# Window attention and its gradients on one core: start-up loads, one weight product and the crossed copies are rearranged

## The chip, the cores and the metric

The kernel runs on one core of a Trainium2 chip. A core has a matrix engine (TensorE, PE in the profile), VectorE (DVE), ScalarE (ACT), GpSimd (POOL) and SyncE (SP), each with an instruction stream of its own. SP, ACT and POOL also issue DMA transfers; SPq, ACTq and POOLq are their issues in the profile. PEld is TensorE loading the stationary operand of its next products. The metric is the device time of one execution in microseconds; less is better.

## The reference

An image of 256 x 256 tokens with 384 channels is cut into windows of 8 x 8 tokens. Each window attends within itself, with one head; then the gradients of all three inputs are formed for a given gradient of the output. Everything is bf16 outside the sums.

```python
# per window (64 tokens), C = 384
qkv = xw @ wqkv                       # q, k, v
p = softmax(q @ k.T * C ** -0.5)
o = (p @ v) @ wo
# outputs: o, and d/dx, d/dwqkv, d/dwo for grad_out
```

## The kernel before, in words

The windows are taken eight at a time: a "quad" is four pairs of vertically adjacent windows (QUAD = 4, 128 tokens a pair), and there are 128 quads. The weights are multiplied out first: A = w_q w_k^T (scaled) and B = w_v w_o, with the transposes AT and BT, so that scores, values and gradients come from x and the output's gradient (dq in the code, with d for its columns) in one product each.

The order of the instructions is the order of the program on all five engines (a manual schedule): each engine takes its instructions as the code lists them and waits where operands or buffers are not ready. All PSUM tiles come from one ring of eight banks.

The main loop (line 490) has 129 iterations i. Each first issues on SP the transposing DMAs dT and xT of quad i+2 (`load_turn`, L151), then `to_tokens` of quad i (L188, tile tok from zy); then `step(c, b, a, ahead)` with c = quad i-1, b = quad i, a = quad i+1 and ahead = quad i+4 lays out one step:

- scores of b on PE (tile sd), then eight products u and v of b (`uv`), copied out of PSUM by ACT, with the softmax parts (`soft`, mostly DVE) in between;
- for the first four quads and the last ("crossed" quads) `stack` has ACT copy P into the tile cr (L246), `soft(…, 5)` has DVE write the gradient of the scores beside it (L239), and `turn` transposes cr by a DMA on SP into PS (L264). cr has one buffer. For the others DVE transposes (L267, L271);
- the projections of a (`project`, three z and three y, copied by ACT at L176 and L178), gathered by DVE into zy (L184);
- from i = 4 on, sums for the weight gradients (tiles pg and ph);
- the attention of c (`attend`, L296): four slots of products pw, pu, po and pd, which need tok and PS of quad c; their results are copied by ACT and DVE and stored by POOL.

`load` (L142 and L144) issues a quad's gradient on POOL and its x on SP, four transfers each.

Ahead of the loop: `fetch_weights` issues w_v and w_o on SP and ACT; seven warm-up products run on PE; POOL builds the identity and clears the accumulator GF_acc; `load_first` issues the gradient of quad 0 on SP and ACT in turn, then `fetch_rest` (w_q on SP, w_k on ACT), then x of quad 0 on SP, and has POOL copy one column of the gradient's last part to the tile spare (L136), so that POOL's loads of quads 1 and on wait until that part has landed. PE then turns w_v, forms BT (`weight_product`, L110), turns the gradient, w_q, projects, turns w_k and x, forms A, and so on. `weight_product` fills one bank after another. w_o is turned for the end of the kernel (`turn_blocks(woT_sb, wo_sb)`) after step 1.

Of the kernel before, what the change touches and what calls it, by code (L numbers as in the profile page):

```python
# [8 lines left out]
ACT = mybir.ActivationFunctionType  # L9
ALU = mybir.AluOpType  # L10
AX = mybir.AxisListType
BF16 = mybir.dt.bfloat16
F32 = mybir.dt.float32

P = 128
WIN = 8
WT = WIN * WIN
QUAD = 4
# [5 lines left out]
def kernel(  # L24
# [21 lines left out]
    nc = tc.nc  # L46
    _, H, W, C = x.shape
    CK = C // P
    J = 3 * C
    JK = J // P  # L50
    scale = float(C) ** -0.5
# [3 lines left out]
    qp = ctx.enter_context(tc.tile_pool(name="qp", bufs=2))  # L55
    sm = ctx.enter_context(tc.tile_pool(name="sm", bufs=2))
    ob = ctx.enter_context(tc.tile_pool(name="ob", bufs=8))
    ring = ctx.enter_context(tc.tile_pool(name="ring", bufs=8, space=bass.MemoryType.PSUM))
# [13 lines left out]
    def columns(k):  # L72
        return slice(k * C, (k + 1) * C)

    def fetch_weights():
        wo_in = wo.rearrange("(m p) n -> p m n", p=P)
        nc.sync.dma_start(out=w_sb[:, 0:2, columns(2)], in_=w_in[:, 0:2, columns(2)])
        nc.scalar.dma_start(out=w_sb[:, 2, columns(2)], in_=w_in[:, 2, columns(2)])
        nc.scalar.dma_start(out=wo_sb[:, 0:2, :], in_=wo_in[:, 0:2, :])
        nc.sync.dma_start(out=wo_sb[:, 2, :], in_=wo_in[:, 2, :])  # L80

    def fetch_rest():
        nc.sync.dma_start(out=w_sb[:, :, columns(0)], in_=w_in[:, :, columns(0)])
        nc.scalar.dma_start(out=w_sb[:, :, columns(1)], in_=w_in[:, :, columns(1)])

    def warm_up(n):
        zero = B_sb[:].rearrange("p m c -> p (m c)")[:, 0:4 * P]
        nc.vector.memset(zero, 0.0)
        for i in range(n):
            pt = ring.tile([P, 4 * P], F32, tag="r", name="warm")  # L90
            nc.tensor.matmul(pt[:], lhsT=zero[:, 0:P], rhs=zero, start=True, stop=True)

    def copy_out(i, out, in_):
        if i % 2:
            nc.scalar.copy(out=out, in_=in_)
        else:
            nc.vector.tensor_copy(out=out, in_=in_)
# [6 lines left out]
            copy_out(k, dst[:, k, :], pt[:])  # L104

    def weight_product(dst, left, right, sc):
        for mr in range(CK):
            pc = ring.tile([P, C], F32, tag="r", name="pc")
            for mc in range(CK):
                nc.tensor.matmul(pc[:], lhsT=left[:, mc, mr * P:(mr + 1) * P], rhs=right[:, mc, :],  # L110
                                 start=(mc == 0), stop=(mc == CK - 1))
            if sc is not None:
                nc.scalar.activation(out=dst[:, mr, :], in_=pc[:], func=ACT.Copy, scale=sc)
            else:
                copy_out(mr, dst[:, mr, :], pc[:])

    def weight_rest():
        turn_blocks(B_sb, BT_sb)
        turn_blocks(AT_sb, A_sb)

    def windows(ap, st, first, count=2):
        row, col = st["at"]
        return ap[0, row + WIN * first:row + WIN * (first + count), col:col + WIN, :]
# [4 lines left out]
    def load_first(st):  # L128
        st["xq"] = xq = grp.tile([P, QUAD, C], BF16, tag="xq", name="xq", bufs=2 * GQ + 5)
        st["dq"] = dq = qp.tile([P, QUAD, C], BF16, tag="dq", name="dq", bufs=6)  # L130
        for t in range(QUAD):
            (nc.sync, nc.scalar)[t % 2].dma_start(out=dq[:, t, :], in_=windows(grad_out, st, 2 * t))
        fetch_rest()
        for t in range(QUAD):
            nc.sync.dma_start(out=xq[:, t, :], in_=windows(x, st, 2 * t))
        nc.gpsimd.tensor_copy(out=spare[:, 0:1], in_=dq[:, QUAD - 1, 0:1])  # L136

    def load(st):
        st["xq"] = xq = grp.tile([P, QUAD, C], BF16, tag="xq", name="xq", bufs=2 * GQ + 5)
        st["dq"] = dq = qp.tile([P, QUAD, C], BF16, tag="dq", name="dq", bufs=6)  # L140
        for t in range(QUAD):
            nc.gpsimd.dma_start(out=dq[:, t, :], in_=windows(grad_out, st, 2 * t))  # L142
        for t in range(QUAD):
            nc.sync.dma_start(out=xq[:, t, :], in_=windows(x, st, 2 * t))  # L144
# [55 lines left out]
    def over_k(ap, n=P):  # L200
        return ap.unsqueeze(2).broadcast_to([n, QUAD, WT])

    def soft(st, step):
        sd = st["sd"]
        if step == 0:
# [35 lines left out]

    def stack(st):
        if st["crossed"]:
            st["cr"] = cr = qp.tile([P, QUAD, 2, WT], BF16, tag="cr", name="cr", bufs=1)
            for w, h in ((0, LO), (1, HI)):
                nc.scalar.copy(out=cr[h, :, w, :], in_=st["Pb"][h, :, :])  # L246

# [87 lines left out]
    def gf_rows(sts, f, ma):  # L335
        pw = ring.tile([P, C], F32, tag="r", name="pg")
        n = len(sts) * QUAD
        for i in range(n):
            st, t = sts[i // QUAD], i % QUAD
            product(pw[:], st["xq"][:, t, ma * P:(ma + 1) * P], st["UW"[f] + "q"][:, t, :], i == 0, i == n - 1)  # L340
        gf_add(f, ma, [pw])
# [23 lines left out]
    def attention(st):  # L365
        halves = gf_halves(*fill.pop(0)) if fill else iter(())
        for t in range(QUAD):
            attend(st, t)
            yield
            for k in range(QUAD):  # L370
                next(halves, None)

    def step(c, b, a, ahead):


        def on(st):
            return (lambda f, *r: f(st, *r)) if st is not None else (lambda f, *r: None)
        C_, B, A = on(c), on(b), on(a)
        if b is not None and c is None:
            weight_rest()  # L380
        B(scores)
        B(soft, 0)
        B(uv, 0, 0)
        B(uv, 0, 1)
        B(soft, 1)
        B(uv, 1, 0)
        B(uv, 1, 1)
        B(soft, 2)
        B(soft, 3)
        B(uv, 2, 0)  # L390
        B(uv, 2, 1)
        B(stack)
        B(uv, 3, 0)
        B(uv, 3, 1)
        B(soft, 4)
        for mo in range(CK):
            A(project, 0, mo)
        B(soft, 5)
        B(turn)
        if ahead is not None:  # L400
            load(ahead)
        A(gather, 0)
        for mo in range(CK):
            A(project, 1, mo)
        for rows in range(1 if a is not None else 2):
            if fill:
                gf_rows(*fill.pop(0))
        slots = attention(c) if c is not None else iter(())
        for t in range(QUAD):
            if t == 2:  # L410
                A(gather, 1)
            next(slots, None)
        for rest in slots:
            pass
# [5 lines left out]
    sts = [{"at": q, "i": i, "crossed": i <= GQ or i == n - 1} for i, q in enumerate(quads)]  # L420
# [41 lines left out]
    with tc.manual_schedule(engines=MANUAL):  # L462
        spare = sm.tile([P, 1], BF16, name="spare", bufs=1)
        fetch_weights()
        warm_up(7)
        make_identity(nc, ident[:])
        nc.gpsimd.memset(GF_acc[:], 0.0)
        load_first(sts[0])
        load(sts[1])
        load(sts[2])  # L470
        load_turn(sts[0])
        load_turn(sts[1])
        turn_blocks(wT[2], w_sb, 2 * CK)
        weight_product(BT_sb, wo_sb, wT[2], None)
        turn_on_pe(sts[0], "dq", "dT")
        turn_blocks(wT[0], w_sb, 0)
        for mo in range(CK):
            project(sts[0], 0, mo)
        turn_blocks(wT[1], w_sb, CK)
        turn_on_pe(sts[0], "xq", "xT")  # L480
        gather(sts[0], 0)
        weight_product(A_sb, wT[0], wT[1], scale)
        turn_on_pe(sts[1], "dq", "dT")
        for mo in range(CK):
            project(sts[0], 1, mo)
        gather(sts[0], 1)
        held = []
        last = None
        get = lambda i: sts[i] if 0 <= i < n else None
        for i in range(n + 1):  # L490
            if 0 <= i < n - 2:
                load_turn(sts[i + 2])
            if 0 <= i < n:
                to_tokens(sts[i])
            if i == 0:
                load(sts[AHEAD - 1])
            step(get(i - 1), get(i), get(i + 1), get(i + AHEAD))
            if i == 1:
                turn_blocks(woT_sb, wo_sb)
            if i > 0:  # L500
                held.append(sts[i - 1])
                sts[i - 1] = None
            if held and i == n:
                last = gf_final(held)
            elif len(held) == GQ:
                fill.extend((held, f, ma) for f in range(2) for ma in range(CK))
                held = []
        while fill:
            gf_rows(*fill.pop(0))
        weight_gradients(last)  # L510
# [30 lines left out]
```

## Time and profile before

| | us |
|---|---|
| median of three runs | 1905.82 |
| the three runs | 1900.98, 1905.82, 1908.59 |
| the profiled execution | 1906.89 |
| its span | 1905.1 |
| PE busy | 1892.1 |
| DVE, ACT, POOL busy | 1667.7, 1526.8, 861.8 |
| mean granted TensorE clock | 0.999 |

The span runs from the first to the last instruction that the profiler recorded; the device time holds 1.79 us more. Times of events are microseconds from the start of the span. A timeline row gives start, duration, engine, source line, operation, destination and source tile, count, and in brackets the idle time before it with what ended that. A row "PE 1892.1 (99%)" says how long an engine worked, as a share of the span; products on PE overlap, so a busy PE is not necessarily at its peak. By issue the DMA part lists, in the first 60 us, x loads of 96 KB landing 3.8 us after their issue in the median, POOL's gradient loads 4.2 us, the four gradient loads of quad 0 on SP and ACT 5.1 and 4.9 us, and the transposes of tok 6.8 us.

### The profile page before, as it was taken

The numbers are of one execution on the slowest core, as the hardware profiler recorded it, in microseconds if no ns is written. First come the engines' busy times: TensorE is split into PE (matmuls) and PEld (weight loads), VectorE is DVE, ScalarE is ACT, GpSimd is POOL, SyncE is SP. The second block draws the span as 40 slices with busy tenths as digits, with TensorE's granted clock in tenths as the row PEclk, the third lists the DMA queues.
The fourth block names the chain that finished last, engine by engine and source line by source line (L and its number), as shares of the span: only waits on it lengthen the run. The fifth ranks groups of instructions, "written<-read, shape, count | busy, mean of one in ns | idle before, by whom it ended". The sixth has DMA issues, their size and how long they took to land.

```text
span 1905.1 us, 57100 instructions
## 1 busy us (share of the span) xinstructions
PE 1892.1 (99%) x22333; PEld 1127.1 (59%) x22333; DVE 1667.7 (88%) x3613; ACT 1526.8 (80%) x3355; POOL 861.8 (45%) x1572
## 2 busy tenths in 40 slices
PE   9999999999999999999999999999999999999999
PEld 5565655655665566556555655665566556556655
DVE  5888888888888888888888888888888888888887
ACT  7877887888788888878887888788788878887884
POOL 4444444444454445444444544444445445444432
PEclk9999999999999999999999999999999999999999
DMA  9999999999999999999999999999999999999994
GB/s 208 218 226 204 219 222 230 217 217 216 223 220 214 222 216 219 218 210 228 216 217 206 228 217 223 217 219 214 220 221 219 217 212 222 223 216 221 195 202 104
DMA packets 949647, 408.34 MB, mean 214 GB/s; under 512 B 831232, under 2 KB 924864, under 8 KB 949376
## 3 DMA queue, kind: packets, MB, share of 16 engines
q1 hardware_dynamic: 873056, 253.08, 77.6%
q0 software_dynamic: 75072, 150.72, 31.4%
q8 instruction: 175, 2.87, 0.6%
q10 hardware_dynamic: 1248, 0.89, 0.2%
q14 instruction: 96, 0.79, 0.1%
HBM read 101.84 MB, written 101.84 MB: 107 GB/s over the span
## 4 chain that ended last, share of the span: by engine, by line
PE 96%; DMA 2%; ACT 1%; DVE 1%; issue 0%; DVEq 0%; ACTq 0%
PE pj L162 51%; PE pg L162 13%; PE ph L351 13%; PE sd L162 5%; PE pw L296 5%; PE pu L296 4%; PE po L296 4%; DMA tok<-zy 1%; PE pd L296 1%; DMA w_sb<-in_wqkv_dram 0%; DMA PS<-cr 0%; PE pe L429 0%; ACT yz L176 0%; ACT yz L178 0%; PE pt L103 0%
## 5 line engine op out<-in xcount | busy, mean ns | idle before, releaser
L316 POOL DMA_DIRECT2D out_dram<-o x512 | 274.5, 536 | 897.3 <-ACT o L300 885.3
L307 ACT CAST Wq<-pw 128x384 bf16<-128x384 f32 x506 | 244.0, 482 | 280.4 <-PE pw L296 280.3
L162 PEld LDWEIGHTS <-xT 128*128 128x128 bf16 x3072 | 291.7, 98 | 182.5 <-issue 0.5
L162 PE MATMUL pj<-B_sb,xT 128*128 128x384 bf16 x1536 | 333.4, 326 | 0.1
L162 PE MATMUL pj<-AT_sb,xT 128*128 128x384 bf16 x1536 | 333.3, 326 | 0.0
L142 POOL DMA_DIRECT2D dq<-in_grad_out_dram x508 | 268.8, 537 | 96.1 <-DMA out_dram<-d 38.3
L310 DVE CAST Uq<-pu 128x384 bf16<-128x384 f32 x512 | 283.1, 553 | 13.2 <-PE pu L296 1.1
L318 POOL DMA_DIRECT2D out_dram<-d x480 | 279.3, 582 | 15.4 <-ACT uq L256 6.8
L162 PE MATMUL pj<-dT,BT_sb 128*128 128x512 bf16 x1152 | 269.5, 379 | 0.0
L162 PE MATMUL pj<-xT,A_sb 128*128 128x512 bf16 x1152 | 269.5, 379 | 0.0
L296 PE MATMUL pd<-tok,ps 64*64 64x384 bf16 x2048 | 257.3, 327 | 1.9 <-DMA tok<-zy 1.5
L176 ACT CAST yz<-pj 128x512 bf16<-128x512 f32 x384 | 224.0, 587 | 36.7 <-PE pj L162 28.4
L300 ACT CAST o<-po 128x384 bf16<-128x384 f32 x512 | 249.8, 488 | 1.5 <-PE po L296 1.1
L256 ACT CAST vq<-pj 128x384 bf16<-128x384 f32 x512 | 247.0, 482 | 3.2
L256 ACT CAST uq<-pj 128x384 bf16<-128x384 f32 x512 | 244.3, 477 | 4.4 <-PE pj L162 2.5
L178 ACT CAST yz<-pj 128x512 bf16<-128x512 f32 x384 | 224.5, 588 | 22.8
L271 DVE STREAM_TRANSPOSE PS<-ps 32x256 bf16<-32x256 bf16 x492 | 214.5, 436 | 9.4
L162 PEld LDWEIGHTS <-xq 128*128 128x128 bf16 x1572 | 153.6, 98 | 115.3 <-issue 0.9
L351 PEld LDWEIGHTS <-xq 64*64 64x64 bf16 x6000 | 176.2, 107 | 67.7
L351 PE MATMUL ph<-Wq,xq 64*64 64x384 bf16 x3984 | 204.5, 322 | 0.0
L162 PEld LDWEIGHTS <-A_sb 128*128 128x128 bf16 x1152 | 112.7, 98 | 135.7
L162 PEld LDWEIGHTS <-BT_sb 128*128 128x128 bf16 x1152 | 112.7, 98 | 122.1
(93 smaller groups left out, 3060.0 us busy)
## 6 DMA issues: line engine op xcount, KB each, us to landing
xq<-in_x_dram SPq DMA_DIRECT2D x512, 96.0 KB, 4.0
out_dram<-o POOLq DMA_DIRECT2D x512, 96.0 KB, 4.0
dq<-in_grad_out_dram POOLq DMA_DIRECT2D x508, 96.0 KB, 5.9
out_dram<-d POOLq DMA_DIRECT2D x480, 96.0 KB, 4.6
out_dram<-d POOLq DMA_DIRECT2D x64, 48.0 KB, 5.1
tok<-zy SPq DMA_TRANSPOSE x128, 7.8
xT<-xq SPq DMA_TRANSPOSE x127, 7.2
dT<-dq SPq DMA_TRANSPOSE x126, 7.9
```

What stands on the lines that cost most here:

```text
L142: nc.gpsimd.dma_start(out=dq[:, t, :], in_=windows(grad_out, st, 2 * t))
L162: nc.tensor.matmul(out, lhsT=lhsT, rhs=rhs, start=start, stop=stop)
L176: ENG[EV["z"][mo]](out=yz[:, mo, :, 0:4:3, :], in_=pj[:])
L178: ENG[EV["y"][mo]](out=yz[:, mo, :, 1:3, :], in_=pj[:])
L256: cp(out=dst[:, t, :], in_=pj[:])
L296: nc.tensor.matmul(dst[o, :], lhsT=operand(st, lhs, t, h), rhs=operand(st, rhs, t, h), **flags)
L300: copies[EV[name][i]](out=sb[rows, :], in_=src[rows, :])
L307: copies[EV["W"][t] if st["i"] >= GQ else "DA"[t % 2]](out=st["Wq"][:, t, :], in_=pw[:])
L310: copies[EV["U"][t]](out=st["Uq"][:, t, :], in_=pu[:])
L316: nc.gpsimd.dma_start(out=windows(out_0, st, 2 * t), in_=o)
L318: nc.gpsimd.dma_start(out=windows(out_1, st, 2 * t - 1), in_=d if t else above[:])
L351: nc.tensor.matmul(dst[o, :], lhsT=st["xq"][h, t, ma * P + o.start:ma * P + o.stop], rhs=st["UW"[f] + "q"][h, t, :], start=(i == 0), stop= ...
```

## The change

There are five edits, all outside the steady part of the loop, save that the last quad is crossed too.

1. The remaining weights (w_q, w_k) are issued within `fetch_weights`, ahead of the gradient of quad 0.
2. The gradient of quad 0 is issued on POOL, four transfers, ahead of the clearing of GF_acc; the copy to spare follows the clearing.
3. `weight_product` takes three banks at once and runs the contraction in its outer loop, so the three banks are complete together; the copies follow.
4. `stack` comes after the last u and v products of its step, and cr has two buffers (the pool's default).
5. w_o is turned after step 0 instead of after step 1.

```diff
     def fetch_weights():
...
         nc.sync.dma_start(out=wo_sb[:, 2, :], in_=wo_in[:, 2, :])
-
-    def fetch_rest():
         nc.sync.dma_start(out=w_sb[:, :, columns(0)], in_=w_in[:, :, columns(0)])
         nc.scalar.dma_start(out=w_sb[:, :, columns(1)], in_=w_in[:, :, columns(1)])
...
     def weight_product(dst, left, right, sc):
+        pcs = [ring.tile([P, C], F32, tag="r", name="pc") for mr in range(CK)]
+        for mc in range(CK):
+            for mr in range(CK):
+                nc.tensor.matmul(pcs[mr][:], lhsT=left[:, mc, mr * P:(mr + 1) * P], rhs=right[:, mc, :],
+                                 start=(mc == 0), stop=(mc == CK - 1))
         for mr in range(CK):
-            pc = ring.tile([P, C], F32, tag="r", name="pc")
-            for mc in range(CK):
-                nc.tensor.matmul(pc[:], lhsT=left[:, mc, mr * P:(mr + 1) * P], rhs=right[:, mc, :],
-                                 start=(mc == 0), stop=(mc == CK - 1))
             if sc is not None:
-                nc.scalar.activation(out=dst[:, mr, :], in_=pc[:], func=ACT.Copy, scale=sc)
+                nc.scalar.activation(out=dst[:, mr, :], in_=pcs[mr][:], func=ACT.Copy, scale=sc)
             else:
-                copy_out(mr, dst[:, mr, :], pc[:])
+                copy_out(mr, dst[:, mr, :], pcs[mr][:])
...
         for t in range(QUAD):
-            (nc.sync, nc.scalar)[t % 2].dma_start(out=dq[:, t, :], in_=windows(grad_out, st, 2 * t))
-        fetch_rest()
+            nc.gpsimd.dma_start(out=dq[:, t, :], in_=windows(grad_out, st, 2 * t))
         for t in range(QUAD):
             nc.sync.dma_start(out=xq[:, t, :], in_=windows(x, st, 2 * t))
-        nc.gpsimd.tensor_copy(out=spare[:, 0:1], in_=dq[:, QUAD - 1, 0:1])
...
-            st["cr"] = cr = qp.tile([P, QUAD, 2, WT], BF16, tag="cr", name="cr", bufs=1)
+            st["cr"] = cr = qp.tile([P, QUAD, 2, WT], BF16, tag="cr", name="cr")
...
-        B(stack)
         B(uv, 3, 0)
         B(uv, 3, 1)
+        B(stack)
...
+        load_first(sts[0])
         nc.gpsimd.memset(GF_acc[:], 0.0)
-        load_first(sts[0])
+        nc.gpsimd.tensor_copy(out=spare[:, 0:1], in_=sts[0]["dq"][:, QUAD - 1, 0:1])
...
-            if i == 1:
+            if i == 0:
                 turn_blocks(woT_sb, wo_sb)
```

## The prediction

> **What bounds the kernel now.** I read the profile in this order: the page's first part, engine use by stage, the chain of work that ended last, then the timelines of ScalarE (ACT), the SP queue and TensorE over the first 100 us. First the page and five stages, cut where the behaviour changes (columns: stretch, length, busy time of PE, weight loads, DVE, ACT, POOL, then granted clock, DMA share, GB/s):
>
> ```profile
> span 1905.1 us, 57100 instructions
> ...
> PE 1892.1 (99%) x22333; PEld 1127.1 (59%) x22333; DVE 1667.7 (88%) x3613; ACT 1526.8 (80%) x3355; POOL 861.8 (45%) x1572
> ...
> 0.00:18.50 18.50, 15.96 (x125) 9.74 (x126) 5.90 (x17) 10.61 (x21) 12.94 (x27) 1.00 0.90 230
> 18.50:71.00 52.50, 47.65 (x420) 25.18 (x417) 39.76 (x93) 41.28 (x95) 16.17 (x30) 0.97 1.03 209
> 71.00:190.50 119.50, 117.76 (x1399) 70.40 (x1396) 103.52 (x225) 94.99 (x208) 54.72 (x100) 1.00 1.15 214
> 190.50:1821.00 1630.50, 1630.43 (x19468) 972.89 (x19471) 1450.48 (x3135) 1325.73 (x2911) 751.96 (x1371) 1.00 1.12 218
> ```
>
> From 190.5 to 1821 us PE is never idle, and its scores start every 14.56 us: 112 steps that no line of the change touches. All it can win is PE's idle time before 190.5 (2.54 + 4.85 + 1.74 = 9.1 us) and whatever the clock lost there. The stall the change aims at is step 2, on ACT and then PE:
>
> ```profile
> 46.40 0.48 ACT L256 CAST vq<-pj 128x384 bf16<-128x384 f32 x1
> 51.28 0.82 ACT L246 COPY cr<-ps 64x256 bf16<-64x256 bf16 x2 [4.40 <-DMA PS<-cr]
> ...
> 52.65 0.32 PE L296 MATMUL pw<-dq,ps 64*64 64x384 bf16 x1 [1.64 <-ACT uq L256]
> ...
> 54.00:56.00 2.00, 1.72 (x16) 0.51 (x16) 1.49 (x3) 2.00 (x5) 0.00 (x0) 0.73 1.18 235
> 56.00:58.00 2.00, 2.00 (x29) 1.62 (x28) 1.94 (x5) 1.69 (x5) 1.41 (x3) 0.50 1.16 218
> ```
>
> ACT stands 4.4 us before the crossed copy, because the one cr buffer is still being read by quad 1's transpose; the last uq and vq and all z and y copies queue behind it, PE idles 1.64 us, and then the clock falls to half. But the queue that feeds PE tells another story:
>
> ```profile
> 39.25 4.96 SPq L188 DMA_TRANSPOSE tok<-zy  x1
> 44.31 3.20 SPq L264 DMA_TRANSPOSE PS<-cr  x1
> 47.57 2.88 SPq L144 DMA_DIRECT2D xq<-in_x_dram  x4
> 50.68 1.45 SPq L151 DMA_TRANSPOSE dT<-dq  x1
> 52.17 1.86 SPq L151 DMA_TRANSPOSE xT<-xq  x1
> 54.14 3.98 SPq L188 DMA_TRANSPOSE tok<-zy  x1
> ...
> L188 SPq EVENT_SEMAPHORE  x4: 27/28/28, 54.1 to 98.9; - x4
> ...
> 84.65 11.45 DMA tok<-zy
> ...
> 172.31 13.57 DMA tok<-zy
> ```
>
> SP issues back to back from 14.53 us on, and its semaphore instructions ahead of a tok transpose last 28 ns: it waits for no engine. tok(1) leaves at 39.25, 12.1 us behind the start of its step (27.18); tok(4) at 84.65 is 13.6 and tok(10) at 172.31 is 13.4 behind (71.04 and 158.94). Those two, each needed by the attention of the step after, are the last two rows, from the chain that ended last: PE waited 1.52 us for tok(10) at 185.92. Only afterwards does SP catch up (12.4 us behind in step 12, 6.4 in step 22). So the start-up is bound by SP's transposes; a faster PE meets them sooner.
>
> **The change part by part.** The profiled execution took 1906.89 us, 1.79 more than its span and 1.07 above the median of 1905.82.
>
> *Loads.* w_q's block goes out on SP right after wo, at about 1.76 instead of 3.84 us, and w_k's on ACT at about 1.7 instead of 3.32: SP and ACT lose two gradient issues each (1.46 and 1.26 us). w_q took 5.9 us to land (9.74), and PE idled 1.34 us for it. It lands between 7.7 (same 5.9 us) and 9.7 (the same bytes share the same engines: 249 and 237 GB/s at 8 to 10 us); I take the middle, -0.7 us of PE idle, and keep 0 and -1.3. x of quad 0 starts on SP at about 2.2 instead of 4.75, but SP held back issues until older loads had landed (0.6, 0.5 and 0.3 us before the w_q block and x), so the third and fourth issue still wait for landings at 3.3 to 3.8, and the next quad's for w_q and w_k. I put x of quad 1 0.7 us earlier; this is the load for which SP's first transpose waited 1.5 us (12.9 to 14.4). That -0.7 shifts the whole SP chain; the bounds are -2.5 (all of x's advance) and 0 from this edit.
>
> *The gradient on POOL.* Four issues at 0.58 us (POOL's median there) from 1.31 to 3.6, then the 2.01 us clearing to 5.6, hidden: POOL stood until 7.61 for the gradient anyway. Gradient loads issued before 14 us took 3.3 to 5.3 us to land, so the last (issued near 3.0) lands at 6.3 to 8.3; before, POOL's copy to spare saw it at 7.61. Everything POOL issues next (20 gradient loads from 7.73) stands behind that copy and moves by -1.3 to +0.7; I take 0. By the Trainium skill (DMA: Bandwidth & Descriptors, Specifications) a load issued by GpSimd has its first byte after about 1 us against 0.6 from SP or ACT; by it the gradient would be 0.4 us later and the sum below 1905.5. No run here shows that figure: the rows have POOL's loads landing no later than SP's (4.2 in the median over 60 us against 5.1), under other traffic.
>
> *w_o w_v in three banks.* The same nine matmuls. For BT_sb the first bank is now complete after seven of them instead of three, but the last copy (7.81 to 8.37) stays: nothing. For A_sb, all three copies are ACT's: they began 0.2 us after the first bank (14.11; matmuls 0.163 apart from 13.42) and now begin at about 14.75, ending near 16.2 instead of 15.58. ACT's dT copies and the three y copies (16.40 to 18.28) queue behind and end up to 0.7 later; quad 0's scores wait for them. Between 0 (PE's B and AT turns stand until 18.66) and +0.7; I take +0.5, being nearer to ACT's queue.
>
> *Crossed copies last, two buffers.* In step 0 ACT waited 0.41 us for ps ahead of cr, with uq and vq behind it: -0.4. In step 1 it stood 1.82 us; the attention stage then took 5.04 us (36.68 to 41.72) against 3.89 in step 3 (67.15 to 71.04): -1.2. In step 2 the 4.4 us stand goes: 16.2 us become step 3's 12.5, -3.7, of which about 1.9 is the halved clock (54.5 to 58.3). Step 3 waited 0.45 with no PE idle: 0. In the last quad the copies end about 0.5 us later on ACT, at 1871.8, but DVE's half of cr is written until 1873.1 and is what the transpose waits for: 0; without that cover it would be +0.5.
>
> *w_o's turn a step earlier.* Nine transposes, 0.64 us of PE between steps 1 and 2 (41.72 to 42.36), move to the end of step 0, where PE waited 0.29 + 0.29 us and more for y copies (27.18 to 28.16). DVE's two turn copies (0.61) then stand before quad 1's row maximum, which had 0.32 us of slack: -0.4 net, bounds -0.64 and 0.
>
> PE alone: -0.7 + 0.5 - 0.4 - 1.2 - 0.4 - 3.7 = **-5.9 us**.
>
> **What is late next.** Step 2 would start at 40.2 (2.2 earlier) and its attention be due 8.6 later, at 48.8. It needs quad 1's turned P and S, issued at 44.31 behind tok(1) and landing 6.9 later, at 51.2: PE idles about 2.4 us there instead. Step 3 starts at 55.1 (57.0 if the clock halves again) instead of 58.56, so step 4 at 67.6 to 69.5, and its attention is due at 78.2 to 80.1; quad 3's transpose lands at 73.28 + 7.1 = 80.4. Step 5's attention began at 96.14 the moment tok(4) landed (84.65 + 11.45 = 96.10). From there PE stands where SP puts it: every microsecond won before is waited for, and what remains is SP's own shift, -0.7 us. Sum: 1905.1 - 0.7 = 1904.4 of span, 1906.2 with the 1.79; on the median's scale 1905.82 - 0.7 = **1905.1 us**.
>
> **The rivals.** *The gain is kept*: SP's issues get shorter when PE's demands move, or tok(4) and tok(10) land earlier. For it: tok issues vary from 3.7 to 7.3 us, tok(10)'s delay follows an odd pair of issues at 164 to 172 (4.18 and 3.64 us), and only 0.5 us was lost at tok(4). Against: back-to-back SP rows. It gives 1905.8 - 5.9 = 1899.9.
> *Slower, by the gradient's landing*: POOL's stream stands behind quad 0's gradient. SP's transpose of quad 2's gradient (17.11) follows the issue of POOL's eighth load (about 11.6) by 5.5 us, hardly more than a landing (up to 5.3). If quad 0's gradient lands later than 7.6 by more than the 0.7 SP wins, SP stands in line there with xT, tok and PS behind it, and the run grows by the excess. With the 6.8 us that POOL's gradient loads took in the median between 14 and 24 us, under full load, it lands at 3.0 + 6.8 = 9.8, so +2.2 - 0.7: 1907.3. It passes the old time from 8.3 on.
> *The two buffers do nothing*, since the wait on cr turns into one on PS at once: that is inside the forecast.
>
> **How the numbers follow.** Forecast 0.62, gain kept 0.20, slower by the gradient 0.15, something outside 0.03. The three runs shown spread from 1900.98 to 1908.59, so each case carries some 3 us either way; 0.5% (9.5 us) is about what a measurement can tell from no change. The range takes in both rivals' centres, the upper with 1.7 us of that spread: 1899.8 to 1909. No case reaches 1896.3 or 1915.3 at its centre; with the spread the kept gain may pass the one (0.04), an unforeseen stall in start-up or loop the other (0.03). Same: 0.93.
>
> **What would show it.** Right: the 4.4 us ACT wait at cr is gone; PE waits for PS<-cr or tok<-zy in steps 2 to 5 instead; tok(10) and tok(11) leave SP within 2 us of 172.3 and 188.5; steps stay at 14.56 us. Wrong: step 12's scores start at 186 or earlier (kept), the transpose of dq on SP begins after 18 us (slower), or the step itself is no longer 14.56.

## The result: 0.5% slower, and TensorE waits for tok

| | before | after |
|---|---|---|
| median of six runs, us | 1905.98 | 1916.17 |
| lowest to highest | 1900.98 to 1908.59 | 1912.13 to 1918.94 |
| ratio, 95% interval | | 1.0054 [1.0036, 1.0072] |
| profiled execution, its span | 1906.89, 1905.1 | 1912.13, 1910.4 |

The forecast was 1905.1 in a range up to 1909.0, so the change cost some 10 us where about none was expected. The profiled execution of the new kernel is the fastest of its six; its trace explains 5.3 us of span, and the other runs lost up to 7 us more in a way that was not traced. Line numbers in the new kernel are lower by three from the loads on (L185 is tok, L261 PS, L148 dT and xT, L139 the gradient loads). From the page of the new kernel:

```profile
span 1910.4 us, 57100 instructions
...
PE 1891.5 (99%) x22333; PEld 1127.3 (59%) x22333; DVE 1667.3 (87%) x3613; ACT 1527.4 (80%) x3355; POOL 862.1 (45%) x1576
```

Its engine use in the same stages as before (stretch, length, busy time of PE, weight loads, DVE, ACT and POOL, then clock, DMA share, GB/s):

```profile
0.00:18.50 18.50, 15.25 (x107) 8.65 (x108) 5.71 (x16) 9.37 (x19) 12.62 (x26) 1.00 0.85 204
18.50:71.00 52.50, 44.65 (x400) 25.09 (x402) 36.97 (x87) 40.53 (x91) 16.40 (x30) 0.93 1.05 194
71.00:190.50 119.50, 115.28 (x1332) 67.97 (x1325) 101.54 (x221) 94.00 (x206) 53.56 (x98) 0.99 1.11 220
190.50:1821.00 1630.50, 1630.50 (x19485) 973.13 (x19483) 1450.42 (x3135) 1325.93 (x2912) 752.01 (x1372) 1.00 1.12 218
```

PE stands idle 7.85 us instead of 4.85 between 18.5 and 71 us, 4.22 instead of 1.74 up to 190.5, and the clock there is lower. Between 190.5 and 1821 us they do not differ. The stall that the change aimed at is gone from ScalarE's timeline: the crossed copy of step 2 follows the last v product at once, where it had stood 4.40 us.

```profile
46.05 0.48 ACT L253 CAST vq<-pj 128x384 bf16<-128x384 f32 x1
46.42 0.82 ACT L243 COPY cr<-ps 64x256 bf16<-64x256 bf16 x2
```

PE's timeline shows what came in its place. These are its waits of over a microsecond between 10 and 110 us:

```profile
10.27 0.34 PE L155 MATMUL pt<-ident,dq 128*128 128x128 bf16 x3 [1.27 <-DMA dq<-in_grad_out_dram]
...
56.68 0.53 PE L293 MATMUL pd<-tok,ps 64*64 64x384 bf16 x2 [6.14 <-DMA tok<-zy]
...
88.61 0.53 PE L293 MATMUL pd<-tok,ps 64*64 64x384 bf16 x2 [3.58 <-DMA tok<-zy]
```

Within the wait of 6.14 us (50.5 to 56.7) the granted clock goes to half, and the first products behind it run at that clock, as the windows around it show:

```profile
50.00:54.00 4.00, 0.55 (x3) 0.10 (x1) 0.00 (x0) 0.83 (x2) 0.00 (x0) 0.99 1.23 143
54.00:58.00 4.00, 1.32 (x19) 1.13 (x23) 1.30 (x3) 0.10 (x1) 0.00 (x0) 0.50 1.20 204
58.00:62.00 4.00, 3.97 (x63) 2.56 (x56) 3.91 (x9) 3.50 (x9) 3.29 (x6) 0.66 1.18 253
```

The chain of work that ended last now leads from the gradient of quad 0 through two tok transposes that land 13.3 and 14.7 us after their issue (start, length):

```profile
3.22 7.00 DMA dq<-in_grad_out_dram
...
43.20 13.34 DMA tok<-zy
...
63.99 6.68 DMA PS<-cr
...
73.87 14.69 DMA tok<-zy
```

On the SP queue the transposes of quad 2's gradient, tok(0) and tok(1) leave 5.2, 2.4 and 4.0 us later than before (17.11, 23.95 and 39.25):

```profile
22.28 1.50 SPq L148 DMA_TRANSPOSE dT<-dq  x1
...
26.38 4.75 SPq L185 DMA_TRANSPOSE tok<-zy  x1
...
43.20 6.60 SPq L185 DMA_TRANSPOSE tok<-zy  x1
```

On POOL, its copy to spare sees the gradient at 10.27 instead of 7.61, and all later gradient loads stand behind it. At 38.88 to 43.16 POOL issues the eight stores of quad 0, the last of them just before tok(1) leaves; in the kernel before, the first store left at 39.76, half a microsecond behind tok(1).

```profile
1.50 2.27 POOL L131 DMA_DIRECT2D dq<-in_grad_out_dram  x4 [0.19 <-issue]
3.73 2.07 POOL L465 MEMSET GF_acc<- 128x2304 f32 x1
10.27 0.19 POOL L466 COPY spare<-dq 128x1 bf16<-128x1 bf16 x1 [4.47 <-DMA dq<-in_grad_out_dram]
10.39 7.51 POOL L139 DMA_DIRECT2D dq<-in_grad_out_dram  x14
...
38.88 0.55 POOL L313 DMA_DIRECT2D out_dram<-o  x1 [13.80 <-ACT o L297]
...
43.16 0.53 POOL L315 DMA_DIRECT2D out_dram<-d  x1
```

The same two places in the kernel before:

```profile
7.61 0.19 POOL L136 COPY spare<-dq 128x1 bf16<-128x1 bf16 x1 [4.34 <-DMA dq<-in_grad_out_dram]
...
39.76 0.55 POOL L316 DMA_DIRECT2D out_dram<-o  x1 [20.24 <-ACT o L300]
```

The length of each step, from one step's first scores to the next's, says where the time went:

| step | before | after | difference |
|---|---|---|---|
| start of step 0 | 18.50 | 19.46 | +0.96 |
| 0 | 8.68 | 9.02 | +0.34 |
| 1 | 15.18 | 12.75 | -2.43 |
| 2 | 16.20 | 19.63 | +3.43 |
| 3 | 12.48 | 13.28 | +0.80 |
| 4 | 14.56 | 19.87 | +5.31 |
| 5 | 15.04 | 14.57 | -0.47 |
| 6 to 11 | 89.77 | 87.39 | -2.38 |
| start of step 12 | 190.41 | 195.97 | +5.56 |

TensorE came to the end of step 1 1.1 us ahead of the old kernel, and lost 9.5 us in steps 2 to 4.

### The profile page after: what moved, and what is told of

Same layout as the page of the kernel before. It is cut to its first block, busy times and chain, and to the rows that moved or that the text cites. A ratio compares the mean times of both kernels' runs of the same rounds, so it can differ in the third digit from the quotient of the medians.

```text
span 1910.4 us, 57100 instructions
## 1 busy us (share of the span) xinstructions
PE 1891.5 (99%) x22333; PEld 1127.3 (59%) x22333; DVE 1667.3 (87%) x3613; ACT 1527.4 (80%) x3355; POOL 862.1 (45%) x1576
## 4 chain that ended last, share of the span: by engine, by line
PE 97%; DMA 2%; DVE 0%; ACT 0%; issue 0%; POOL 0%; POOLq 0%
PE pj L159 51%; PE pg L159 13%; PE ph L348 13%; PE sd L159 5%; PE pw L293 5%; PE pu L293 4%; PE po L293 4%; DMA tok<-zy 1%; PE pd L293 1%; DMA dq<-in_grad_out_dram 0%; DMA PS<-cr 0%; PE pe L426 0%; PE pt L101 0%; DVE Uq L307 0%; POOL dq L131 0%
## 5 line engine op out<-in xcount | busy, mean ns | idle before, releaser
L139 POOL DMA_DIRECT2D dq<-in_grad_out_dram x508 | 268.5, 539 | 91.0 <-DMA out_dram<-o 24.6
L315 POOL DMA_DIRECT2D out_dram<-d x480 | 278.2, 580 | 12.6 <-ACT uq L253 5.1
L297 ACT CAST o<-po 128x384 bf16<-128x384 f32 x512 | 249.5, 487 | 10.2 <-PE po L293 9.6
```

The lines of the kernel that those rows point to most:

```text
L297: copies[EV[name][i]](out=sb[rows, :], in_=src[rows, :])
L315: nc.gpsimd.dma_start(out=windows(out_1, st, 2 * t - 1), in_=d if t else above[:])
```

## The experiments

Two theories were set against each other. *Late landing*: the gradient, now issued among the weights, lands late and pushes POOL's and SP's streams. *Run-ahead*: without the stand at cr, attention ends earlier, its eight stores (96 KB each) reach the DMA engines ahead of SP's tok transpose, and tok lands so late that TensorE loses more than it had won. All runs are five rounds against the kernel before, on the chip that they ran on themselves; its median there was 1906.12 for the first four, 1905.11 for the next four, 1904.90 for the last four.

### Half of the change at a time

**e1_undo_loads**: the new kernel with the old start-up loads.

```diff
+    def fetch_rest():
...
-            nc.gpsimd.dma_start(out=dq[:, t, :], in_=windows(grad_out, st, 2 * t))
+            (nc.sync, nc.scalar)[t % 2].dma_start(out=dq[:, t, :], in_=windows(grad_out, st, 2 * t))
+        fetch_rest()
```

> The changed kernel with the loads of before: quad 0's gradient on SP and ACT, w_q and w_k behind it, clearing first (three banks, late crossed copies, two buffers and w_o's early turn are kept). Load theory (the gradient on POOL lands at 10.3 instead of 7.6 us, so POOL's stream and with it SP's transpose of quad 2's gradient is late, 22.3 instead of 17.1, and everything SP issues behind it): back to 1904 to 1906 us, SP's dT at 17, tok of quad 1 leaves near 39. Run-ahead theory (ScalarE no longer stalls, TensorE is ahead, its stores enter the DMA engines ahead of tok, and tok lands late): still 1912 or more, with TensorE waiting over 4 us for tok in step 2.

1909.76 us, 1.0023 [1.0012, 1.0033]: between the times of the two theories. In its trace, of an execution of 1915.24 us, TensorE waits 4.20 us for tok in step 2, as run-ahead has it.

**e2_loads_only**: the kernel before with the new loads (edits 1 and 2).

```diff
-            (nc.sync, nc.scalar)[t % 2].dma_start(out=dq[:, t, :], in_=windows(grad_out, st, 2 * t))
-        fetch_rest()
+            nc.gpsimd.dma_start(out=dq[:, t, :], in_=windows(grad_out, st, 2 * t))
```

> The kernel before with the two load edits alone (w_q and w_k early, quad 0's gradient on POOL ahead of the clearing). Load theory: 1912 to 1917 us, SP's dT of quad 2 at about 22. Run-ahead theory: 1905 to 1908, since the crossed copies still hold ScalarE and TensorE back.

1907.59 us, 1.0012 [1.0002, 1.0022], in run-ahead's range and below the load theory's. Yet the transpose of quad 2's gradient leaves SP at 20.86 and tok(0) at 26.37, about as late as in the new kernel. With cr in one buffer the stores still come behind tok(1), the first by 0.56 us.

**e3_stack_only**: the kernel before with the late crossed copies, the two buffers and w_o's earlier turn (edits 4 and 5).

```diff
-            st["cr"] = cr = qp.tile([P, QUAD, 2, WT], BF16, tag="cr", name="cr", bufs=1)
+            st["cr"] = cr = qp.tile([P, QUAD, 2, WT], BF16, tag="cr", name="cr")
...
-        B(stack)
         B(uv, 3, 0)
         B(uv, 3, 1)
+        B(stack)
...
-            if i == 1:
+            if i == 0:
                 turn_blocks(woT_sb, wo_sb)
```

> The kernel before with the late crossed copies, two buffers for cr and w_o's early turn, and nothing else. Load theory, and my prediction's chain: 1903 to 1906 us, the 4.4 us wait of ScalarE gone, TensorE waiting for PS or tok instead. Run-ahead theory: 1910 or more. If the gain were kept: 1900 to 1901.

1911.82 us, 1.0029 [1.0020, 1.0038]. Here the gradient lands as before and SP's tok(1) leaves as before, at 39.29, yet the kernel is 5.7 us slower. Its timeline: the stores now lie ahead of tok(1), the issue on SP takes 7.25 instead of 4.96 us, tok lands 13.1 instead of 10.6 us later, and TensorE stands 4.20 us.

```profile
36.99 0.55 POOL L316 DMA_DIRECT2D out_dram<-o  x1 [18.18 <-ACT o L300]
...
39.29 7.25 SPq L188 DMA_TRANSPOSE tok<-zy  x1
...
41.27 0.53 POOL L318 DMA_DIRECT2D out_dram<-d  x1
...
52.48 0.53 PE L296 MATMUL pd<-tok,ps 64*64 64x384 bf16 x2 [4.20 <-DMA tok<-zy]
```

So both theories hold a part. The crossed copies and buffers cost 5.7 us by themselves, the loads 1.5, and the whole change 10.2. By the medians that is more than their sum, but the intervals (0.20 to 0.38% and 0.02 to 0.22%, against 0.36 to 0.72%) do not show it. Since e1, which adds the three banks to the edits of e3, is no slower than it, the banks cost nothing that can be measured; they were not tried alone.

**e4_no_gate**: the new kernel without POOL's copy to spare, so that POOL's loads of the next quads do not wait for quad 0's gradient.

```diff
-        nc.gpsimd.tensor_copy(out=spare[:, 0:1], in_=sts[0]["dq"][:, QUAD - 1, 0:1])
```

> The changed kernel without POOL's copy to spare: POOL issues the gradients of quads 1 and on from 5.8 us, without standing until quad 0's has landed. If the late gate is what moves SP: dT of quad 2 on SP back to 17 to 18 us and 1904 to 1908 us in all. If the loads are late because the DMA engines are shared by more transfers at once: dT still at 20 to 22 and 1912 or more, quad 0's gradient even later than 10.3.

1911.23 us, 1.0028 [1.0017, 1.0040]. The transpose of quad 2's gradient leaves SP at 16.28, earlier than in the kernel before, but the time does not come back to the 1904 to 1908 us that were expected with it. About 5 us of the loss went with the wait (the two intervals barely overlap), and what stays is the size of e1's and e3's. The late gradient thus hurts through POOL's stream behind it.

### Which of the stack's edits

**e5_two_bufs**: the kernel before with the second cr buffer alone.

```diff
-            st["cr"] = cr = qp.tile([P, QUAD, 2, WT], BF16, tag="cr", name="cr", bufs=1)
+            st["cr"] = cr = qp.tile([P, QUAD, 2, WT], BF16, tag="cr", name="cr")
```

> The kernel before with two buffers for cr and nothing else. Run-ahead theory (without ScalarE's stand of 4.4 us TensorE finishes steps 1 and 2 sooner, its stores and POOL's next loads go out earlier, share the DMA engines with SP's transposes, and these take longer): most of the loss of the late-copies kernel, 1909 to 1912 us. Rival (the order of ScalarE's copies or w_o's early turn costs): 1906.

1910.07 us, 1.0023 [1.0013, 1.0034]. One buffer more, and with it the end of the 4.4 us stand, costs 5 us. The stores of quad 1 begin at 51.67, tok(2) leaves behind four of them and takes 15.0 us to land; TensorE stands 6.1 us for it. The traced execution took 1906.59 us, though, and starts step 12 at 190.31 us, where the trace of before has 190.41: it won 4.0 us in steps 1 and 2 and lost 6.9 in step 3. So the trace shows what the late tok does in one step; the loss of 5 us is that of the medians. From SP's and PE's timelines:

```profile
53.73 7.97 SPq L188 DMA_TRANSPOSE tok<-zy  x1
...
68.76 0.53 PE L296 MATMUL pd<-tok,ps 64*64 64x384 bf16 x2 [6.10 <-DMA tok<-zy]
```

**e6_stack_last**: the kernel before with the crossed copies behind the last v products, one buffer.

```diff
-        B(stack)
         B(uv, 3, 0)
         B(uv, 3, 1)
+        B(stack)
```

> The kernel before with the crossed copies behind the last u and v copies, cr still in one buffer and w_o turned after step 1. The stand at cr stays but now holds only the z and y copies. Run-ahead theory: about as before, 1904 to 1908 us, since ScalarE still waits for PS<-cr in step 2. Rival (the order costs): 1909 or more.

1905.60 us, 1.0012 [1.0000, 1.0024]: no loss, or one below what can be told. ScalarE's stand for the one buffer is still there, 6.3 us, and TensorE is held back as before (steps 1 and 2 take 14.68 and 18.22 us). So the loss of e3 goes with the second buffer, though the interval leaves room for some of it in the later copies.

### Stores ahead of tok, or behind

**e7_hold_stores**: e3, with POOL kept busy between the first and the second store of quads 0 to 2. GF_acc is still all zero then, so two more clearings change nothing but the time.

```diff
             nc.gpsimd.dma_start(out=windows(out_0, st, 2 * t), in_=o)
+        if t == 0 and st["i"] < 3:
+            for k in range(2):
+                nc.gpsimd.memset(GF_acc[:], 0.0)
```

> The late-copies kernel (two buffers, late crossed copies, w_o's early turn) in which POOL clears GF_acc twice more (about 4.1 us) between the first and the second store of quads 0, 1 and 2, so that SP's tok enters the DMA engines ahead of the stores. Run-ahead theory: tok of quad 1 lands in 10 to 11 us instead of 13, less waiting in steps 2 and 3, 1904 to 1908 us. Rival (SP's transposes are slow for another reason than the stores beside them): no better than the late-copies kernel, 1911 to 1913.

1906.17 us, 1.0004 [0.9995, 1.0014]: the loss is gone. tok(1) leaves with one store ahead of it instead of four, its issue takes 4.69 us and it lands after 8.1 us instead of 13.1; tok(2) after 6.6 instead of 13.3. The landing of tok(1) in the kernel before, in e3 and in e7:

```profile
DMA to landing us min/median/max: 10.6/10.6/10.6
...
DMA to landing us min/median/max: 13.1/13.1/13.1
...
DMA to landing us min/median/max: 8.1/8.1/8.1
```

The timeline of e7:

```profile
38.17 4.41 POOL L319 MEMSET GF_acc<- 128x2304 f32 x2
...
38.28 4.69 SPq L188 DMA_TRANSPOSE tok<-zy  x1
...
42.53 0.59 POOL L323 DMA_DIRECT2D out_dram<-d  x1
```

The experiment is not as clean as it was meant to be. While POOL cleared, VectorE's gather into zy took 1.99 us; in e3 it took 0.55. First e7, then e3:

```profile
38.63 1.99 DVE L184 COPY zy<-yz 128x1536 bf16<-128x1536 bf16 x1
```

```profile
37.99 0.55 DVE L184 COPY zy<-yz 128x1536 bf16<-128x1536 bf16 x1
```

The attention's copies behind the gather came later too, TensorE waited 1.85 us for them in each of the three steps, and step 1 became 14.2 us long against 12.76 in e3. So the hold both moves the stores and slows TensorE. It also moves the gradient loads that POOL issues behind the stores: the first leaves at 46.25, at the end of tok(1)'s landing, and in e3 at 41.98, within it. That tok lands sooner is thus the doing of POOL's held transfers, the stores first among them; that the total comes out even is a sum of a gain and a new loss.

**e8_pe_turns_stack**: e3, with two transposes taken off SP: TensorE turns x of quad 1 and the gradient of quad 2 (it already turned x of quad 0 and the gradients of quads 0 and 1). SP then reaches each tok sooner, ahead of the stores, without any hold.

```diff
-    G_ON_PE, X_ON_PE = 2, 1
+    G_ON_PE, X_ON_PE = 3, 2
...
+        turn_on_pe(sts[1], "xq", "xT")
...
+            if i == 0:
+                turn_on_pe(sts[2], "dq", "dT")
```

> The late-copies kernel in which TensorE also turns x of quad 1 and the gradient of quad 2, so SP issues two transposes less (14.5 and 17.1 us before; 2.3 and 3.7 us of its queue). If SP's queue bounds the start-up, tok of quad 0 leaves SP at about 19 instead of 23 to 24 us, the waits for tok and PS in steps 2 to 4 shrink by as much, and 1900 to 1905 us result: faster than both kernels. If what holds TensorE is the sharing of the DMA engines by stores and loads later on: 1908 to 1912.

1901.36 us, 0.9984 [0.9975, 0.9994]. tok(1) leaves at 34.78, 3.7 us ahead of the first store, and lands after 6.4 us. Steps 1 to 3 take 12.46, 12.48 and 12.48 us, what the prediction had put for step 2 without the stand. But tok leaves later in every step: 0.45 us after the step's first scores in step 0, 6.4, 8.5, 10.5, 12.3 and 12.8 in the next five, until step 7 takes 21.24 us with a wait for tok. In this execution SP's transposes bind after all; a TensorE at full pace only reaches that bound later. It took 1906.30 us, 4.9 above the median, so executions near the median can hardly have held a stall of that size (step 7 is 6.7 us longer than the usual 14.56). From the timelines of SP, POOL and PE:

```profile
34.78 4.72 SPq L188 DMA_TRANSPOSE tok<-zy  x1
...
38.51 0.54 POOL L316 DMA_DIRECT2D out_dram<-o  x1 [19.81 <-ACT o L300]
...
125.55 0.53 PE L296 MATMUL pd<-tok,ps 64*64 64x384 bf16 x2 [3.76 <-DMA tok<-zy]
```

Over all kernels the landing of tok(1), tok(2) and tok(3) goes by its order against the stores. From the timelines of SP and POOL and the landings, for the eleven kernels without the hold (33 transposes):

| first of the eight stores leaves | transposes | landing, us | median |
|---|---|---|---|
| 1.2 us or more behind tok | 9 | 6.4 to 8.9 | 7.7 |
| up to 0.6 us behind tok | 5 | 8.6 to 10.6 | 10.2 |
| ahead of tok | 19 | 9.9 to 16.4 | 12.6 |

### The change as a whole, and a better one

**e9_after_hold**: the new kernel with the hold of e7.

```diff
+        if t == 0 and st["i"] < 3:
+            for k in range(2):
+                nc.gpsimd.memset(GF_acc[:], 0.0)
```

> The changed kernel with POOL's two extra clearings (about 4.1 us) between the first and second store of quads 0, 1 and 2, as in the late-copies kernel with held stores. If its loss is the sum of the stores' sharing (some 4 to 6 us) and the loads' lateness: 1907 to 1911 us, and tok of quad 1 lands in under 11 us instead of 13.3. If the late gradient alone makes the loss once TensorE no longer stalls at cr: still 1914 or more.

1906.78 us, 1.0009 [1.0001, 1.0018]. The gradient still lands late (11.16) and quad 2's transpose still leaves SP late (20.98), but tok(1) lands after 8.6 us instead of 13.3. Some 8 of the 10 us go when the stores are held; the 1.9 left are about what the loads cost alone (1.5), but the price of the hold is in them too (e12).

**e10_grad_on_sp**: the new kernel with quad 0's gradient on SP and ACT in turn, still behind w_q and w_k.

```diff
-            nc.gpsimd.dma_start(out=dq[:, t, :], in_=windows(grad_out, st, 2 * t))
+            (nc.sync, nc.scalar)[t % 2].dma_start(out=dq[:, t, :], in_=windows(grad_out, st, 2 * t))
```

> The changed kernel with quad 0's gradient on SP and ACT again, but behind w_q and w_k, all else as changed. If what delays the gradient is that w_q, w_k and x now share the DMA engines with it: it lands at 9 to 10 us here too, SP's transpose of quad 2's gradient leaves at 19 us or later, 1912 to 1916 us. If it is POOL's issue itself: at 8 us or sooner, 17 to 18 us, 1908 to 1911 us, as with all load edits undone.

1914.34 us, 1.0044 [1.0031, 1.0057], not to be told from the new kernel. The gradient was in at 9.22, still 1.6 us later than before, and tok(1) left at 43.70, again behind all eight stores. So it is not mainly GpSimd's issuing that costs, but at least in good part that the loads stand among the weights and x. One expectation failed: quad 2's transpose left SP at 18.26, not at 19 or later and only 1.1 us later than before. tok(1) came late because SP's issues in between took longer (tok(0) 6.19 us against 4.40, the x of quad 3 3.95 against 1.87), so a late gradient is not the only way to put it behind the stores.

**e11_pe_turns**: the kernel before with the two turns on TensorE (the diff of e8 without e3's edits), one cr buffer.

```diff
-    G_ON_PE, X_ON_PE = 2, 1
+    G_ON_PE, X_ON_PE = 3, 2
```

> The kernel before with x of quad 1 and the gradient of quad 2 turned on TensorE, two transposes fewer on SP, and the stand at cr kept. SP's chain is up to 5 us earlier in step 0, so PS of quad 1 lands sooner and ScalarE's stand at cr shrinks: 1900 to 1904 us. If most of the gain of the same kernel with two buffers comes from the freed ScalarE once SP keeps up: 1903 to 1906.

1899.60 us, 0.9975 [0.9966, 0.9985]: faster than the kernel before by 5.3 us, and than the new one by some 15.5 (10.2 and 5.3, each against its own runs of the kernel before). On SP tok(0) and tok(1) leave 4.2 and 3.7 us earlier than before:

```profile
19.79 3.99 SPq L188 DMA_TRANSPOSE tok<-zy  x1
...
35.55 4.69 SPq L188 DMA_TRANSPOSE tok<-zy  x1
```

Its engine use shows most of the idle time gone (2.60 us from 18.5 to 71, none from there to 190.5), for 24 more products on PE:

```profile
18.50:71.00 52.50, 49.90 (x479) 27.89 (x477) 42.40 (x99) 44.48 (x103) 18.16 (x33) 0.97 1.02 203
71.00:190.50 119.50, 119.50 (x1412) 71.36 (x1411) 105.50 (x230) 97.61 (x216) 54.74 (x101) 1.00 1.16 220
```

ScalarE's stand at cr, at which the change had been aimed, went away by itself: SP's earlier transposes free the one buffer in time, and the copy of step 2 (47.08) no longer waits for it.

**e12_pe_turns_hold**: e8 with the hold of e7.

```diff
+        if t == 0 and st["i"] < 3:
+            for k in range(2):
+                nc.gpsimd.memset(GF_acc[:], 0.0)
```

> The kernel with TensorE's two turns and the late, doubly buffered crossed copies, with POOL's two extra clearings (about 4.1 us) between the first and second store of quads 0, 1 and 2. If the stores beside SP's transposes are still what holds it back in steps 1 to 3: 1897 to 1900 us. If SP now keeps ahead there and is overtaken only later (steps 5 to 8): 1901 to 1903, no better than without.

1906.74 us, 1.0012 [1.0003, 1.0020], some 5.5 us slower than e8. With tok already ahead of the stores its landing has nothing to gain (6.6 us for tok(1) against 6.4 in e8), so this run shows the price of the hold: TensorE waits 5.5 us in all, in three places, for VectorE's copies. The traces of e7 and e9 have the same three waits, and steps 1 to 3 take 43.7 and 43.6 us there, 43.4 here and 37.4 in e8. So e7 and e9 pay some 6 us for the hold as well. What the held order gave back must then be more than the 5 and 8 us by which their totals fell, if gain and price simply add, which no run shows.

## Why the prediction was wrong

*What bounds the start-up: right.* SP's transposes do: two fewer of them won 3.7 us in e8 and 5.3 in e11. All four signs that were named for a right forecast came true (no wait at cr, waits for tok and PS in steps 2 to 4, tok(10) and tok(11) at 173.63 and 188.16, steps of 14.56 us), and so did the sign for the slower rival (the transpose of dq at 22.28, after 18). The first four hold for a late landing as well and could not tell it from the forecast.

*TensorE's own gains: right in size.* For steps 0 and 1 the terms -0.4, -1.2 and -0.4 came to -2.0; measured -2.09. The closeness is in part luck: step 0, for which the terms leave -0.4 and at most the 0.24 us that the moved turn still costs, grew by 0.34, and step 1 lost 2.43, against the 1.2 and 0.64 that were to leave it. The -3.7 of step 2 is borne out by e8, whose step 2 takes 12.48 us.

*Ahead of step 0: wrong by 1.2 us.* The terms -0.7 and +0.5 came to -0.2; step 0 started 0.96 later. TensorE no longer waited for w_q (1.34 us before), but 0.41, 0.20 and 1.27 us for the gradient. The three banks cost about 0.1 and not 0.5: from A's first product to quad 0's scores it took 5.17 us instead of 5.08.

*The step that failed: "From there PE stands where SP puts it: every microsecond won before is waited for, and what remains is SP's own shift, -0.7 us."* That takes SP's issue times and landings as fixed. They are not: attention that ends earlier sends its stores earlier. The list of what is late next leaves out tok(1), and so takes its old 10.6 us from issue to landing for the new kernel as well; e3, with the same issue time, has 13.1, and its issue alone holds SP 2.3 us longer, with everything else on SP behind it. The prediction looked for TensorE's wait in step 2 to end at 51.2 with PS; in the new kernel it ended at 56.5 with tok, at half the clock. The stand at cr, counted as pure loss, had kept the stores behind tok. That the order is the cause of the late landing is shown by e7 (the same edits, stores held: 13.1 to 8.1 us, and the loss gone) with the table of landings; how much of the 5 us is the landing, how much SP's longer issues and how much the halved clock was not separated. Nor does PE stand where SP puts it from there on: tok(10) and tok(11) leave SP within 1.4 us of their old times, but TensorE, 5.6 us late by step 12, no longer waits for them.

By the Trainium skill (DMA: Bandwidth & Descriptors, Issuing engines are not separate DMA queues) transfers started by SP, ACT and GpSimd run on the same 16 engines and interleave, whoever started them. The runs agree: the same transpose lands after 6.4 us or 13 to 16 by where another engine's stores stand. The rule was there to be applied to the stores that move.

*A second term mis-sized: the gradient on POOL, "I take 0".* The bounds for POOL's stream were -1.3 to +0.7 us; measured +2.66 (7.61 to 10.27). The landing was taken as 3.3 to 5.3 us from loads in the old order; the chain shows 7.00, now that the weights ahead of them share the engines. The rival "slower, by the gradient's landing" had this mechanism and, with a landing at 9.8, 1907.3 us; e2, the loads alone, gave 1907.59, with the gradient in at 10.96; that the size fits so well is partly luck. What it lacked was the other edit: late transposes on SP put tok(1) at 43.20, behind all eight stores, where e3 had it behind four. Its chance of 0.15 was too small, since a range that is bounded by old landings leaves out that the order of the loads was the thing changed.

*SP's shift of -0.7 from the loads* came only at SP's first transpose, of quad 1's x, which left 1.3 us earlier (13.20); the next one waited for its gradient and left 5.2 us later, tok(0) 2.4.

## What to carry to other kernels

A stall on one engine can be what keeps another engine's transfers in order, so before removing it list which transfers will move earlier and what they will then share the DMA engines with; a landing time read from a trace holds only for the order that it was measured in. If the queue of one engine bounds a stage, take work off that queue rather than speed up whoever waits for it: here two transposes moved to TensorE gave 0.25%, while a second buffer cost 0.23%. And a move of loads has to be priced at its new place in the crowd, with the waits that gate other streams on its landing.

## What the runs showed of the hardware that was not expected

- A tok transpose on SP takes 3.7 to 8.3 us to issue and 5.5 to 16.4 us to land in these kernels' first 95 us; with plain stores of another engine ahead of it both grow (e3: 4.96 to 7.25 and 10.6 to 13.1 us at the same moment).
- A GpSimd clearing of 128x2304 f32 held up VectorE's copy from SBUF to SBUF (0.55 to 1.99 us), while its copies out of PSUM stayed at 0.54 to 0.56. The Trainium skill (SBUF — State Buffer, Who interferes with whom) says that VectorE in a two-port mode and GpSimd lock each other out for a whole instruction and that copies can enter such a mode; the 1.99 us beside a clearing of some 2.2 us agree.
- Within TensorE's wait of 6.14 us (50.5 to 56.7) the granted clock fell: it was 0.99 from 50 to 54 us, 0.50 from 54 to 58 and 0.66 from 58 to 62, so it came back some 4 us after the wait had ended. No long wait was needed elsewhere: in the kernel before, an idle time of 1.64 us came shortly ahead of the windows at 0.73 and 0.50, and in e11 the clock was at 0.50 for 3.41 us although PE had been busy for 2.72 of the 3.41 us ahead of them, with no gap above 0.14 us. Step 3 of e11 took 14.15 us, against 12.46 for its step 2:

```profile
63.17:66.58 3.41, 2.72 (x29) 1.03 (x29) 2.04 (x4) 3.41 (x9) 0.00 (x0) 1.00 1.19 246
66.58:69.99 3.41, 3.35 (x48) 2.24 (x44) 2.98 (x7) 2.88 (x8) 3.39 (x7) 0.50 1.11 207
```
